# Clustered attention and a routed expert layer on one core: four places in a hand-written order of work are moved

## The chip, the cores and the metric

The kernel runs on one core of one Trainium2 chip. A core has a matrix engine (TensorE, PE in the profile; its weight loads are PEld), VectorE (DVE), ScalarE (ACT), GpSimd (POOL) and SyncE (SP), which here only issues DMA transfers. Each engine works through its own list of instructions in order and waits at an instruction until the semaphores that it needs have come. TensorE writes to PSUM, which VectorE and ScalarE read. Times are device microseconds (us) of one launch, lower is better.

## The reference

The first half is attention over clusters. For each of 4 batches and 8 heads (768 tokens, 64 columns a head), each query and each key is given to the most similar of 16 centroids, and a query may look only at keys of its own cluster:

```python
q_assign = np.argmax(np.einsum('bhsd,hcd->bhsc', q_n, c_n), axis=-1)
k_assign = np.argmax(np.einsum('bhsd,hcd->bhsc', k_n, c_n), axis=-1)
mask = q_assign[:, :, :, None] == k_assign[:, :, None, :]
scores = scale * np.matmul(q, k.transpose(0, 1, 3, 2))
scores = np.where(mask, scores, -1000000000.0)
scores = scores - np.max(scores, axis=-1, keepdims=True)
attn = np.exp(scores)
attn = attn / (np.sum(attn, axis=-1, keepdims=True) + 1e-09)
return np.matmul(attn, v).astype(np.float32)
```

The second half takes the 3072 rows of 512 columns that come out. Rows with a positive `x @ w_skip` go to one of 8 experts (the largest of `x @ w_gate`), a two-layer network with 1024 hidden columns, and `gate * result` is added to the row; the others pass unchanged. All data are float32.

## The kernel before, in words

**Pairs and tiles.** Two heads of one batch make a *pair*, so there are 16 pairs (0 to 15). A pair has 24 *score tiles*: 2 halves of 384 queries, 6 blocks of 128 keys, 2 heads. "Tile 7.16" is tile 16 of pair 7, counted from 0. For a tile, `score` issues two products into a PSUM tile `ps` (lines L553 and L554: the rounded high parts and mask rows, and the low-part corrections), ScalarE takes the exponential into `PT` (L556), and GpSimd adds the `PT` of a half up in `acc` (L561, L567; the last pair of them on VectorE). There are two `ps` buffers, so tile n can only start when the exponential of tile n-2 is done. Twice in a half, six `PT` at a time, `avs` multiplies by V into one PSUM tile `av` (L578, six products that the trace counts as 12, called an av block here). A pair's blocks stand behind its tiles 7 and 13 (first half) and 19 and the next pair's tile 1 (second half). When a half is through, `vm` and `oT` (L591, L592) are the reading of `av` by ScalarE; there is a single `av` buffer, so the next half's first block waits for it.

**What is prepared for later pairs.** Between the tiles stands the work for the next two or three pairs:

- `load` (L346): the `raw` tile, Q and K transposed, 768 KB, two buffers; `load_v` (L354) loads V.
- `sims` (L431): similarities to the centroids, copied to `ss` (L438 on ScalarE, L436 on VectorE for the first pair).
- `assign`: five VectorE steps on `ss` turned round (L462 on TensorE): largest (L444), equal (L447), weight (L450), largest weight (L453), and the one-hot rows `oh` (L455). The generator yields between them, and numbers of the table say how many tiles lie between.
- `masks`: the *mask product*, three small products of `oh` (L474), ScalarE's scaling into `mk` (L478), and eight DMAs of 24 KB (L486) that put 16 rows each into `QM` (queries) and `KB` (keys): four for `QM`, then four for `KB`.
- `split_hi` (L376, L379): rounded high parts `hi`, and DMAs of 192 KB into rows 0 to 63 of `QM` and `KB`; `split_lo` (L386) and `copies` (L395, L396): low parts, and eight DMAs into `qc` and `kc`.
- `smax` (L515, L517): before the scores of a pair, the largest score of every query. 24 products `sm`, one beside nearly every score tile, each reduced by VectorE into `M`; three `sm` buffers. The first of a pair needs the `hi` rows and the mask rows of `QM` and `KB`.
- `mneg` (L528), `mrows` (L536, L541): the *maxima's rows*. VectorE joins the maxima in `MX`, TensorE turns them round, ScalarE writes them into two rows of both `QM` (L541, twice).
- `sums`, `recip`, `xout` (L602 with `sr` L605; L613 with `rs` L618; L639 with `x` L644 and `out` L653): the sums of the previous pair, their reciprocals, and its output turned round, scaled and stored.

The small products (`sims`, `sums`, `mrows`, `recip`, `xout`, `assign`, `masks`, routing) share a PSUM pool `x_ps` of two buffers: such a product waits until the reader of the tile two before it is done. In pairs 5, 9 and 13 (and 4, 8, 12) routing work of the batch before stands in between as well, mostly VectorE's.

**What sets the order.** Nothing is scheduled by the machine. `tasks` gives each function a place in tiles relative to its pair, from the table `PLAN`; `FIRST` replaces some numbers for the first three pairs. `steps` takes the tasks in order of these places and issues their instructions, so a larger number puts an instruction further down the list of its engine. A `yield` inside a function puts the rest of it down later by that many tiles. `zero_rows` sets rows 64 to 95 of four `QM` tiles to zero once, before the first pair.

The expert half follows (L1018 to L1181): gathers of rows by indirect DMA, and three products each for hidden and output layers. The change touches no line of it.

Of the kernel before, what the change touches and what calls it, by code (L numbers as in the profile page):

```python
# [12 lines left out]
F32 = mybir.dt.float32  # L13
# [4 lines left out]
AF = mybir.ActivationFunctionType  # L18
ALU = mybir.AluOpType
# [24 lines left out]


PLAN = {
    "load": -60.0, "load_v": -45.0, "weights": 72.0, "sims": -42.9, "assign": (-34.45, 0.07, 0.04, 0.04, 0.04, 1.6),
    "hi": (-34.3, -28.3), "masks": (-31.1, 0.6), "lo": (-28.35, -16.35), "copies": -16.3, "smax": (-21.1, 1.0, -0.4),
    "mneg": (-9.0, 3.2), "mrows": ((-4.5, 0.2, 0.05), (5.5, 0.8, 0.3)),
    "av": 1.6, "acc": 25.62, "sums": 29.2, "recip": 31.5, "xout": ((31.52, 0.1), (43.55, 0.08)),  # L50
    "tail": ((16.0, 16.6, 19.2), (28.5, 28.6, 29.3)),
    "route": (29.25, 34.9, 58.9), "early": (86.5, 100.9),
    "rtail": ((5.3, 10.9, 16.2, 17.5, 21.5, 18.2, 23.6, 24.2), (5.35, 10.92, 29.1, 29.2, 29.4, 29.5)),
# [6 lines left out]
FIRST = {  # L60
    0: {
        "load_v": -18.9, "sims": -20.0, "hi": (-19.9, -19.8, -19.7, -19.6), "assign": (-19.0, 0.1, 0.01, 0.01, 0.01, 0.01),
        "lo": (-18.7, -18.6, -16.9, -16.8), "masks": -17.0, "smax": (-14.0, 0.1, 13.0, 0.75), "mneg": (-12.85, 8.7),
        "mrows": ((-12.8, 0.1, 0.0), (9.2, 0.0, 0.0)),
    },
    1: {
        "sims": -42.2, "hi": (-42.4, -42.3), "lo": (-40.1, -40.0), "copies": -39.9, "assign": (-36.83, 13.2, 1.3, 1.3, 1.3, 1.3),
        "masks": (-17.6, 0.1), "smax": (-14.5, 1.0, 0.0, 0.92), "mneg": (-2.3, 8.2), "mrows": ((-1.6, 0.1, 0.2), (8.8, 0.3, 0.3)),
    },
    2: {  # L70
        "smax": (-16.0, 0.95, 0.0), "mneg": (-5.2, 6.3), "mrows": ((-4.5, 0.2, 0.05), (7.4, 0.3, 0.3)),
    },
}

# [3 lines left out]
class Kernel:  # L78
# [203 lines left out]
    def tasks(self, i):  # L282

        p, last = {**PLAN, **FIRST.get(i, {})}, i == self.npair - 1
        r = [(s, lambda s=s: self.score(i, s)) for s in range(NS)]
        add = lambda t, f, *a: r.append((t, lambda: f(i, *a)))
        if i:
            add(p["load"], self.load)
        add(p["load_v"], self.load_v)
        if i in (1, 2):  # L290
            add(-20.1 - i * NS, self.zero_rows)
        add(p["sims"], self.sims)
        add(p["assign"][0], self.assign, *p["assign"][1:])
# [12 lines left out]
        for n in range(24):
            add(t0 + dt * n if n < 12 else t0 + 12 * dt + gap + dt2 * (n - 12), self.smax, n)
        for hf in range(2):
            add(p["mneg"][hf], self.mneg, hf)
            add(p["mrows"][hf][0], self.mrows, hf, *p["mrows"][hf][1:])  # L310
            for g in range(0, KT, GROUP):
                add(12 * hf + 2 * (g + GROUP) + p["av"], self.avs, hf, range(g, g + GROUP))
        if not last:
            add(p["sums"], self.sums, (0, 1))
            add(p["recip"], self.recip)
            for hf in range(2):
                add(p["xout"][hf][0], self.xout, hf, p["xout"][hf][1])
        else:
            for hf in range(2):
                t = p["tail"][hf]  # L320
                add(t[0], self.sums_last, hf)
                add(t[1], self.recip_last, hf)
                add(t[2], self.xout_last, hf)
        if i == self.npair - HP - 1:
            for t, f in zip(p["early"], (self.early_lists, self.early_rows)):
                add(t, f)
        if last:
            for hf in range(2):
                ts = p["rtail"][hf]
# [26 lines left out]
    def zero_rows(self, i):  # L356

        for a in range(2):
            self.nc.vector.memset(self.QM[i][a].bitcast(F32)[64:96, :], 0.0)

    def operands(self, i):
        c = self.st[i]
# [206 lines left out]
    def avs(self, i, hf, kts):  # L569
        c, nc = self.st[i], self.nc  # L570
        if kts[0] == 0:
            c["av"] = self.ps_av.tile([P, HALF + 1], F32, name="av")
        av = c["av"]
        first = None
        for kt in kts:
            for a in range(2):

                nc.tensor.matmul(av[a * D:(a + 1) * D, :], lhsT=c["vt"][:, kt, a * D:(a + 1) * D],  # L578
                                 rhs=self.pt(i, hf * 2 * KT + kt * 2 + a), start=(kt == 0), stop=(kt == KT - 1),
                                 skip_group_check=True)  # L580
                if not first:
                    first = self.newest()
                    self.tc.add_manual_dep(first, c[f"exp{hf}{kts[-1]}"].name, mybir.DependencyInfo(
                        mybir.DependencyClass.Sync, mybir.DependencyReason.DATA), reason="group")
        if kts[-1] == KT - 1:
            if hf == 0:
                c["oT"] = self.work.tile([P, S], F32, name="oT", bufs=5)
            if i < self.npair - 1 or hf == 0:
                yield 1.0
            vm = self.small.tile([P, 1], F32, name="vm")  # L590
            nc.scalar.activation(out=vm, in_=av[:, HALF:], func=AF.Copy)  # L591
            nc.scalar.activation(out=c["oT"][:, hf * HALF:(hf + 1) * HALF], in_=av[:, :HALF],  # L592
                                 func=AF.Identity, bias=vm)
            self.out_mark = self.newest()

    def sums(self, i, hfs):

# [719 lines left out]
```

## Time and profile before

| what | value |
|---|---|
| time, three runs | 743.0 us median (742.95 to 744.28) |
| profiled execution, its own time | 743.75 us |
| its span, first to last instruction | 742.0 us |
| mean granted TensorE clock | 0.976 |
| TensorE busy | 679.9 us, 92% of the span |
| VectorE / ScalarE / GpSimd busy | 72% / 53% / 44% |

The span divides into a start of about 25 us without score tiles, some 495 us with them, about 31 us for most pairs, and some 220 us of experts. In a row of the timeline the first number is the start in us, the second the length; brackets hold the idle time before and what ended it. A wait row reads: engine and instruction that waited, what it waited for, us in total, times, longest. "L474" is line 474 of the kernel before; numbers of the changed file run up to 8 higher from line 594 on.

### The profile page before, as it was taken

The page shows a single profiled execution, that of the slowest core. Times are in us where ns is not written, and L with a number is a line of the kernel's source. Part 1 is how long each engine was busy: PE and PEld are TensorE (multiplying, and loading weights), DVE is VectorE, ACT ScalarE, POOL GpSimd, SP SyncE. Part 2 cuts the span into 40 slices and gives each one's busy share as a digit, 9 for nine tenths or more (in the row PEclk, how much of TensorE's full clock was granted, in tenths as well). Part 3 has the DMA queues.
Part 4 walks back from the last instruction along what each step waited for, and adds up shares of the span by engine and source line. Part 5 has one row for each costly group of instructions (what it writes and reads, how often), then busy time and mean ns, then how long its engine had stood idle before and what let it go on. Part 6 is the DMA issues. An engine that isn't in the chain of part 4 may idle for free. (4 is left out here: it accounts for less than half of the span.)

```text
span 742.0 us, 12111 instructions
## 1 busy us (share of the span) xinstructions
PE 679.9 (92%) x3961; PEld 474.1 (64%) x3961; DVE 531.8 (72%) x1072; ACT 390.5 (53%) x793; POOL 329.7 (44%) x355
## 2 busy tenths in 40 slices
PE   4699999999999999989999999899799999999995
PEld 2455665656556565656665655555578988998883
DVE  7565777758889786888885888885667975667711
ACT  6254556656555565655656555573455455455520
POOL 7455545645456454554564544653342222221001
PEclk9889999999999999999999999999899999999998
DMA  8432647557665475563754653331256666667520
GB/s 224 139 76 65 158 115 201 144 140 189 171 200 134 127 181 122 141 153 102 171 133 113 159 130 95 86 130 36 74 195 218 228 215 237 198 217 243 176 71 29
DMA packets 54351, 110.14 MB, mean 148 GB/s; under 512 B 8615, under 2 KB 22823, under 8 KB 54288
## 3 DMA queue, kind: packets, MB, share of 16 engines
q1 hardware_dynamic: 50832, 101.73, 49.0%
q0 software_dynamic: 2656, 7.24, 2.9%
q8 instruction: 32, 0.52, 0.3%
q10 hardware_dynamic: 800, 0.39, 0.2%
q14 instruction: 31, 0.25, 0.1%
HBM read 61.00 MB, written 10.62 MB: 97 GB/s over the span
## 5 line engine op out<-in xcount | busy, mean ns | idle before, releaser
L556 ACT ACTIVATE PT<-ps 128x384 f32<-128x384 f32 x384 | 183.6, 492 | 187.5 <-PE ps L554 167.9
L517 DVE TENSOR_REDUCE M<-sm 128x1 f32<-128x384 f32 x384 | 205.2, 554 | 92.4 <-PE sm L515 88.4
L567 POOL TENSOR_TENSOR acc<-acc,PT 128x384 f32<-128x384 f32 x217 | 202.0, 951 | 121.2 <-ACT PT L556 121.0
L553 PE MATMUL ps<-QM,KB 98*128 98x384 f32 x384 | 149.8, 390 | 5.3 <-ACT PT L556 3.9
L515 PE MATMUL sm<-KB,QM 96*128 96x384 f32 x384 | 139.4, 369 | 4.8 <-DVE M L517 3.1
L578 PE MATMUL av<-PT,vt 128*64 128x385 f32 x768 | 141.5, 504 | 0.0
L554 PE MATMUL ps<-qc,kc 128*128 128x384 f32 x384 | 132.3, 344 | 0.0
L553 PEld LDWEIGHTS ps<-QM,KB 98*128 98x128 f32 x384 | 73.3, 191 | 57.5 <-ACT PT L556 28.5
L561 POOL TENSOR_TENSOR acc<-PT 128x384 f32<-128x384 f32 x64 | 58.4, 913 | 114.0 <-ACT vm L591 104.0
L515 PEld LDWEIGHTS sm<-KB,QM 96*128 96x128 f32 x384 | 75.5, 197 | 29.4 <-issue 10.9
L578 PEld LDWEIGHTS av<-PT,vt 128*64 128x64 f32 x768 | 50.3, 139 | 60.6 <-issue 60.3
L554 PEld LDWEIGHTS ps<-qc,kc 128*128 128x128 f32 x384 | 74.0, 193 | 0.1
L944 POOL DMA_INDIRECT out<-yo,idw x15 | 19.2, 1281 | 112.5 <-DVE yo L1072 101.0
L1048 PE MATMUL ph<-x2l,w1h 128*128 128x256 f32 x224 | 63.6, 284 | 1.6 <-DVE x2l L1060 1.6
L1049 PE MATMUL ph<-x2h,w1h 128*128 128x256 f32 x224 | 63.5, 284 | 0.0
L1050 PE MATMUL ph<-x2h,w1l 128*128 128x256 f32 x224 | 63.4, 283 | 0.0
L1124 DVE SCALAR_TENSOR_TENSOR hl<-ph,hh 128x256 fp32r<-128x256 f32 x56 | 23.7, 423 | 38.5 <-ACT hh L1123 38.4
L1123 ACT ACTIVATE hh<-ph 128x256 fp32r<-128x256 f32 x56 | 21.5, 383 | 47.9 <-PE ph L1050 47.8
L1048 PE MATMUL py<-w2l,hh 128*128 128x512 f32 x112 | 45.1, 403 | 0.0
L1048 PEld LDWEIGHTS ph<-x2l,w1h 128*128 128x128 f32 x224 | 42.9, 192 | 2.1 <-DVE x2l L1060 1.8
L1050 PE MATMUL py<-w2h,hl 128*128 128x512 f32 x112 | 43.7, 390 | 0.0
L1049 PE MATMUL py<-w2h,hh 128*128 128x512 f32 x112 | 43.7, 390 | 0.0
(260 smaller groups left out, 1003.9 us busy)
## 6 DMA issues: line engine op xcount, KB each, us to landing
wraw<-w SPq DMA_DIRECT2D x72, 512.0 KB, 4.6
raw<-qk SPq DMA_DIRECT2D x16, 768.0 KB, 5.5
vt<-v SPq DMA_DIRECT2D x16, 384.0 KB, 4.2
QM<-hi SPq DMA_DIRECT2D x30, 192.0 KB, 6.4
KB<-hi SPq DMA_DIRECT2D x30, 192.0 KB, 3.1
kc<-hi SPq DMA_DIRECT2D x30, 192.0 KB, 3.6
kc<-raw SPq DMA_DIRECT2D x30, 192.0 KB, 3.4
qc<-hi SPq DMA_DIRECT2D x30, 192.0 KB, 3.6
```

The source lines that it names most:

```text
L515: nc.tensor.matmul(sm, lhsT=c["qm"][a][0:96, j * P:(j + 1) * P], rhs=c["kb"][a][0:96, hf * HALF:(hf + 1) * HALF], start=True, stop=True)
L517: nc.vector.tensor_reduce(out=c["m"][:, j, a, hf:hf + 1], in_=sm, axis=AX.X, op=ALU.max)
L553: nc.tensor.matmul(ps, lhsT=c["kb"][a][0:98, ks], rhs=c["qm"][a][0:98, sl], start=True, stop=False)
L554: nc.tensor.matmul(ps, lhsT=c["kc"][a][:, ks], rhs=c["qc"][a][:, sl], start=False, stop=True)
L556: nc.scalar.activation(out=pt, in_=ps, func=AF.Exp, scale=D ** -0.5)
L561: nc.gpsimd.tensor_tensor(out=acc, in0=self.pt(i, s - 2)[:, :HALF], in1=pt, op=ALU.add)
L567: (nc.vector if dve else nc.gpsimd).tensor_tensor(out=acc, in0=acc, in1=pt, op=ALU.add)
L578: nc.tensor.matmul(av[a * D:(a + 1) * D, :], lhsT=c["vt"][:, kt, a * D:(a + 1) * D], rhs=self.pt(i, hf * 2 * KT + kt * 2 + a), start=(kt = ...
L1048: nc.tensor.matmul(ps, lhsT=ah, rhs=bl, start=first, stop=False)
L1049: nc.tensor.matmul(ps, lhsT=ah, rhs=bh, start=False, stop=False)
L1050: nc.tensor.matmul(ps, lhsT=al, rhs=bh, start=False, stop=last)
L1124: nc.vector.scalar_tensor_tensor(out=hl[:, f, :], in0=ph, scalar=0.0, in1=hh.bitcast(F32)[:, f, :], op0=ALU.max, op1=ALU.subtract)
```

## The change

Six edits, in the program's words; nothing is added to or taken from what is computed:

1. `PLAN["assign"]`: the last step (`oh`, L455) is yielded 4.8 tiles instead of 1.6 after the fourth; `PLAN["masks"]`: the mask product goes from place -31.1 to -27.05, and ScalarE's `mk` follows 0.3 instead of 0.6 tiles later. In a pair this is from tile 16 to tile 20.
2. `PLAN["oT"]`: reading `av`. For the first half `vm` and `oT` come 4.5 tiles after the last av block instead of 1.0, still on ScalarE. For the second half `vm` stays on ScalarE, and `oT` becomes a VectorE instruction (add of a scalar per row), 3.55 tiles after the block. The last pair's second half is as before.
3. `PLAN["mrows"]`: the second half's maxima's rows are written 0.1 and 0.05 tiles after their product, not 0.8 and 0.3.
4. `FIRST[2]["load"]`: the third pair's `raw` is requested at place -64.75 instead of -60.
5. `FIRST[0]["smax"]`, `["mneg"]`, `["mrows"]`: pair 0's second twelve maxima come 0.6 instead of 0.75 tiles apart, and what follows them about a tile sooner.
6. `zero_rows` is issued on GpSimd, not on VectorE, and five tiles later.

```diff
-    "load": -60.0, ... "assign": (-34.45, 0.07, 0.04, 0.04, 0.04, 1.6),
-    ... "masks": (-31.1, 0.6), ...
-    "mneg": (-9.0, 3.2), "mrows": ((-4.5, 0.2, 0.05), (5.5, 0.8, 0.3)),
-    "av": 1.6, "acc": 25.62, ...
+    "load": -60.0, ... "assign": (-34.45, 0.07, 0.04, 0.04, 0.04, 4.8),
+    ... "masks": (-27.05, 0.3), ...
+    "mneg": (-9.0, 3.2), "mrows": ((-4.5, 0.2, 0.05), (5.5, 0.1, 0.05)),
+    "av": 1.6, "oT": (4.5, 3.55), "acc": 25.62, ...
@@ FIRST
-    0: ... "smax": (-14.0, 0.1, 13.0, 0.75), "mneg": (-12.85, 8.7), "mrows": ((-12.8, 0.1, 0.0), (9.2, 0.0, 0.0)),
+    0: ... "smax": (-14.0, 0.1, 13.0, 0.6), "mneg": (-12.85, 7.55), "mrows": ((-12.8, 0.1, 0.0), (8.2, 0.1, 0.0)),
-    2: "smax": (-16.0, 0.95, 0.0), ...
+    2: "load": -64.75, "smax": (-16.0, 0.95, 0.0), ...
@@ tasks
-            add(-20.1 - i * NS, self.zero_rows)
+            add(-15.0 - i * NS, self.zero_rows)
@@ zero_rows
-            self.nc.vector.memset(self.QM[i][a].bitcast(F32)[64:96, :], 0.0)
+            self.nc.gpsimd.memset(self.QM[i][a].bitcast(F32)[64:96, :], 0.0)
@@ avs, behind the last block of a half
-            if i < self.npair - 1 or hf == 0:
+            last, oT = i == self.npair - 1, c["oT"][:, hf * HALF:(hf + 1) * HALF]
+            if not last or hf == 0:
                 yield 1.0
             vm = self.small.tile([P, 1], F32, name="vm")
-            nc.scalar.activation(out=vm, in_=av[:, HALF:], func=AF.Copy)
-            nc.scalar.activation(out=c["oT"][...], in_=av[:, :HALF], func=AF.Identity, bias=vm)
+            if not last and hf:
+                nc.scalar.activation(out=vm, in_=av[:, HALF:], func=AF.Copy)
+                yield p[hf] - 1.0
+                nc.vector.tensor_scalar(out=oT, in0=av[:, :HALF], scalar1=vm, scalar2=None, op0=ALU.add)
+            else:
+                if not last:
+                    yield p[hf] - 1.0
+                nc.scalar.activation(out=vm, in_=av[:, HALF:], func=AF.Copy)
+                nc.scalar.activation(out=oT, in_=av[:, :HALF], func=AF.Identity, bias=vm)
```

**Place one: ScalarE, from tile 8.19 to tile 9.6.** `QM_172` and `QM_173` are the two query tiles of the pair that gets its maxima's rows, `PT` the exponentials, `ex` a step of the routing. Before:

```order
L541 ACTIVATE QM_172<-x_ps 2x384
L541 ACTIVATE QM_173<-x_ps 2x384
L556 ACTIVATE PT<-ps 128x384 x7
L591 ACTIVATE vm<-av 128x1
L592 ACTIVATE oT<-av,vm 128x384
L556 ACTIVATE PT<-ps 128x384 x3
L438 ACTIVATE ss<-x_ps 128x384
L605 ACTIVATE sr<-x_ps 128x384
L556 ACTIVATE PT<-ps 128x384
L802 ACTIVATE ex<-ex 128x48
L541 ACTIVATE QM_172<-x_ps 2x384
L541 ACTIVATE QM_173<-x_ps 2x384
```

And with the change:

```order
L541 ACTIVATE QM_172<-x_ps 2x384
L541 ACTIVATE QM_173<-x_ps 2x384
L556 ACTIVATE PT<-ps 128x384 x2
L478 ACTIVATE mk<-x_ps,mbias,mscale 128x384
L556 ACTIVATE PT<-ps 128x384 x5
L594 ACTIVATE vm<-av 128x1
L556 ACTIVATE PT<-ps 128x384 x3
L438 ACTIVATE ss<-x_ps 128x384
L613 ACTIVATE sr<-x_ps 128x384
L541 ACTIVATE QM_172<-x_ps 2x384
L541 ACTIVATE QM_173<-x_ps 2x384
L556 ACTIVATE PT<-ps 128x384
```

`mk` now stands between the exponentials of tiles 21 and 22, `oT` of the second half is gone from ScalarE, and the second pair of `QM` rows stands directly behind `sr`, in front of one exponential and of `ex`.

**Place two: TensorE and SP around the mask product of pair 9, in pair 7.** TensorE before, from tile 7.16 on (`QM_176` and `KB_182` are the operands of pair 8's maxima):

```order
L553 MATMUL ps<-QM_174,KB_180 128x384
L554 MATMUL ps<-qc_2526,kc_2528 128x384
L515 MATMUL sm<-KB_182,QM_176 128x384
L474 LDWEIGHTS oh
L474 MATMUL x_ps<-ident_bf,oh 128x128
L474 LDWEIGHTS oh
L474 MATMUL x_ps<-ident_bf,oh 128x128
L474 LDWEIGHTS oh
L474 MATMUL x_ps<-ident_bf,oh 128x128
L553 MATMUL ps<-QM_175,KB_181 128x384
```

TensorE with the change, from the av block behind tile 7.19 on:

```order
L578 MATMUL av<-PT,vt 64x385 x6
L553 MATMUL ps<-QM_174,KB_180 128x384
L554 MATMUL ps<-qc_2526,kc_2528 128x384
L515 MATMUL sm<-KB_183,QM_177 128x384
L474 LDWEIGHTS oh
L474 MATMUL x_ps<-ident_bf,oh 128x128
L474 LDWEIGHTS oh
L474 MATMUL x_ps<-ident_bf,oh 128x128
L474 LDWEIGHTS oh
L474 MATMUL x_ps<-ident_bf,oh 128x128
L553 MATMUL ps<-QM_175,KB_181 128x384
```

SP's list of transfers in the same stretch of a later pair, before:

```order
L379 DMA QM_176<-hi 64x768
L379 DMA QM_177<-hi 64x768
L486 DMA QM_176<-mk 16x384 x2
L486 DMA QM_177<-mk 16x384 x2
L486 DMA KB_182<-mk 16x384 x2
L486 DMA KB_183<-mk 16x384 x2
L379 DMA KB_182<-hi 64x768
L379 DMA KB_183<-hi 64x768
L653 DMA out<-x 128x3x128
L354 DMA vt<-v 128x768
```

And with the change:

```order
L379 DMA QM_176<-hi 64x768
L379 DMA QM_177<-hi 64x768
L379 DMA KB_182<-hi 64x768
L379 DMA KB_183<-hi 64x768
L661 DMA out<-x 128x3x128
L486 DMA QM_176<-mk 16x384 x2
L486 DMA QM_177<-mk 16x384 x2
L486 DMA KB_182<-mk 16x384 x2
L486 DMA KB_183<-mk 16x384 x2
L354 DMA vt<-v 128x768
```

The product moved past four tiles and an av block, and the eight transfers of mask rows moved behind the two of `KB`'s `hi` rows and one store.

**Place three: SP at the start, the copies of pair 1 and the third `raw`.** `kc_295` and `qc_293` are pair 1's low-part operands for the first head. Before:

```order
L379 DMA KB_180<-hi 64x768
L379 DMA KB_181<-hi 64x768
L395 DMA kc_295<-hi 64x768
L396 DMA kc_295<-raw 64x768
L395 DMA qc_293<-hi 64x768
L396 DMA qc_293<-raw 64x768
L395 DMA kc_296<-hi 64x768
L396 DMA kc_296<-raw 64x768
L395 DMA qc_294<-hi 64x768
L396 DMA qc_294<-raw 64x768
L346 DMA raw<-qk 128x1536
L354 DMA vt<-v 128x768
```

And with the change:

```order
L379 DMA KB_180<-hi 64x768
L379 DMA KB_181<-hi 64x768
L346 DMA raw<-qk 128x1536
L395 DMA kc_293<-hi 64x768
L396 DMA kc_293<-raw 64x768
L395 DMA qc_291<-hi 64x768
L396 DMA qc_291<-raw 64x768
L395 DMA kc_294<-hi 64x768
L396 DMA kc_294<-raw 64x768
L395 DMA qc_292<-hi 64x768
L396 DMA qc_292<-raw 64x768
L354 DMA vt<-v 128x768
```

The load moved in front of eight copies. In the changed program it waits for the readers of the first `raw`, of which GpSimd's subtraction (L414) is the last.

More of the change, by code (lines that the diff above doesn't have):

```diff
@@ L46 @@
 PLAN = {
-    "load": -60.0, "load_v": -45.0, "weights": 72.0, "sims": -42.9, "assign": (-34.45, 0.07, 0.04, 0.04, 0.04, 1.6),
-    "hi": (-34.3, -28.3), "masks": (-31.1, 0.6), "lo": (-28.35, -16.35), "copies": -16.3, "smax": (-21.1, 1.0, -0.4),
-    "mneg": (-9.0, 3.2), "mrows": ((-4.5, 0.2, 0.05), (5.5, 0.8, 0.3)),
-    "av": 1.6, "acc": 25.62, "sums": 29.2, "recip": 31.5, "xout": ((31.52, 0.1), (43.55, 0.08)),
+    "load": -60.0, "load_v": -45.0, "weights": 72.0, "sims": -42.9, "assign": (-34.45, 0.07, 0.04, 0.04, 0.04, 4.8),
+    "hi": (-34.3, -28.3), "masks": (-27.05, 0.3), "lo": (-28.35, -16.35), "copies": -16.3, "smax": (-21.1, 1.0, -0.4),
+    "mneg": (-9.0, 3.2), "mrows": ((-4.5, 0.2, 0.05), (5.5, 0.1, 0.05)),
+    "av": 1.6, "oT": (4.5, 3.55), "acc": 25.62, "sums": 29.2, "recip": 31.5, "xout": ((31.52, 0.1), (43.55, 0.08)),
     "tail": ((16.0, 16.6, 19.2), (28.5, 28.6, 29.3)),
@@ L62 @@
         "load_v": -18.9, "sims": -20.0, "hi": (-19.9, -19.8, -19.7, -19.6), "assign": (-19.0, 0.1, 0.01, 0.01, 0.01, 0.01),
-        "lo": (-18.7, -18.6, -16.9, -16.8), "masks": -17.0, "smax": (-14.0, 0.1, 13.0, 0.75), "mneg": (-12.85, 8.7),
-        "mrows": ((-12.8, 0.1, 0.0), (9.2, 0.0, 0.0)),
+        "lo": (-18.7, -18.6, -16.9, -16.8), "masks": -17.0, "smax": (-14.0, 0.1, 13.0, 0.6), "mneg": (-12.85, 7.55),
+        "mrows": ((-12.8, 0.1, 0.0), (8.2, 0.1, 0.0)),
     },
@@ L70 @@
     2: {
-        "smax": (-16.0, 0.95, 0.0), "mneg": (-5.2, 6.3), "mrows": ((-4.5, 0.2, 0.05), (7.4, 0.3, 0.3)),
+        "load": -64.75, "smax": (-16.0, 0.95, 0.0), "mneg": (-5.2, 6.3), "mrows": ((-4.5, 0.2, 0.05), (7.4, 0.3, 0.3)),
     },
@@ L585, in avs @@
         if kts[-1] == KT - 1:
+            p = PLAN["oT"]
             if hf == 0:
                 c["oT"] = self.work.tile([P, S], F32, name="oT", bufs=5)
-            if i < self.npair - 1 or hf == 0:
+            last, oT = i == self.npair - 1, c["oT"][:, hf * HALF:(hf + 1) * HALF]
+            if not last or hf == 0:
                 yield 1.0
             vm = self.small.tile([P, 1], F32, name="vm")
-            nc.scalar.activation(out=vm, in_=av[:, HALF:], func=AF.Copy)
-            nc.scalar.activation(out=c["oT"][:, hf * HALF:(hf + 1) * HALF], in_=av[:, :HALF],
-                                 func=AF.Identity, bias=vm)
-            self.out_mark = self.newest()
+            if not last and hf:
[7 more added lines that the diff above has]
+                nc.scalar.activation(out=oT, in_=av[:, :HALF], func=AF.Identity, bias=vm)
+                self.out_mark = self.newest()
     def sums(self, i, hfs):
```

## The prediction

> **What bounds the kernel now.** I read the page first, then the list of waits by TensorE, then the timeline at the places that the change touches. A wait row gives the engine and its instruction, what ended the wait, us in total, times, longest.
>
> ```profile
> span 742.0 us, 12111 instructions
> ...
> PE x_ps L474 <- DVE oh L455: 9.1, 15, 0.9
> ...
> PE x_ps L639 <- ACT QM L541: 6.0, 9, 0.7
> ...
> PE x_ps L431 <- DMA raw<-qk: 5.4, 1, 5.4
> ...
> PE x_ps L536 <- DVE MX L528: 3.3, 5, 2.1
> ...
> PE x_ps L639 <- DVE rs L618: 3.0, 5, 0.7
> ...
> PE sm L515 <- DMA KB<-hi: 1.5, 3, 0.7
> ```
>
> TensorE is the busy engine, so in the attention part its own waits are what the end can gain from. The first three rows are 20.5 us, and each stands at an instruction that the change moves or feeds sooner. The other engines' waits are far longer and cost nothing by themselves. What a removed wait is worth depends on what is late next: ScalarE (an exponential for every tile) or VectorE (a reduction for every tile).
>
> **The change, part by part.** All terms are against the profiled execution (743.75 us: the span of 742.0 and 1.75 around it); the median of the runs, 743.0, lies 0.75 below it.
>
> *Start.* The timeline, start and length; in the two rows of windows the fields behind the length are the busy time of PE, PEld, DVE, ACT and POOL with counts, the granted TensorE clock, the DMA share and GB/s.
>
> ```profile
> 6.02 1.93 PE L431 MATMUL x_ps<-raw,cb 128*32 128x384 f32 x8 [0.86 <-DVE cb L227]
> 6.67 3.12 DVE L359 MEMSET QM<- 32x768 f32 x4 [0.20 <-issue]
> 16.75 6.28 DVE L517 TENSOR_REDUCE M<-sm 128x1 f32<-128x384 f32 x12 [0.48 <-PE sm L515]
> 18.24 1.81 POOL L414 TENSOR_TENSOR kc<-raw,kc 64x768 fp32r<-64x768 f32 x1
> 20.13 3.60 POOL L386 TENSOR_TENSOR raw<-raw,hi 128x768 fp32r<-128x768 f32 x2
> 27.20 1.68 POOL L561 TENSOR_TENSOR acc<-PT 128x384 f32<-128x384 f32 x2 [3.47 <-ACT PT L556]
> 28.98 0.55 SPq L346 DMA_DIRECT2D raw<-qk  x1
> 34.78 1.51 PE L431 MATMUL x_ps<-raw,cb 128*32 128x384 f32 x8 [5.39 <-DMA raw<-qk]
> 39.26 2.48 SPq L486 DMA_DIRECT2D QM<-mk  x4
> 44.82 0.34 PE L553 MATMUL ps<-QM,KB 98*128 98x384 f32 x1
> 30.60:34.80 4.20, 0.02 (x3) 0.05 (x4) 0.56 (x2) 0.00 (x0) 0.74 (x1) 0.51 0.83 287
> 34.80:42.50 7.70, 7.54 (x31) 3.59 (x32) 2.08 (x4) 2.15 (x4) 1.85 (x2) 0.60 0.06 16
> ```
>
> The first pair's similarities end at 7.95, but VectorE's copy of them stands behind the four memsets, which end at 9.79. On GpSimd the memsets leave that copy free: **−1.8** (bounds 0, if GpSimd, where no memset of this size is shown, holds up something, and −1.8). Their cover is GpSimd's idle 3.47 us ahead of its first sums at 27.20. It is of much the same length as VectorE's 3.12 us for them; if each took twice as long, the sums would start some 3 us later, and nothing on TensorE waits for those.
>
> The third load is issued at 28.98 behind eight copies that wait for GpSimd's subtraction L386 (to 23.73); TensorE then stands 5.39 us at the similarities that need it. In the new order it needs only L414 (to 20.05, less the 1.8), so with the same 5.8 us from issue to landing (28.98 to 34.78) the data lie there near 24, well before TensorE's turn. SP waits at the load until then, and only the eight copies of pair 1 and a load of V are queued behind it, which waited for GpSimd longer before. The wait goes, and so does the cause of the low clock behind it: 0.60 granted over 7.7 us is about 3.1 us lost. Together that is 8.5 us. VectorE takes part of it back: tile 10 of pair 0 at 44.82 needs the mask rows of pair 1, these VectorE's one-hots, and ahead of those stand nine reductions at 6.28/12 = 0.52 and the five one-hot steps. I put the tile at about 39.8: **−5.0** (−3.5, if VectorE's queue leaves the rows only that much sooner, to −8.5). Pair 0's second maxima, issued a little closer together, are part of this stretch: each is the same product and the same 0.52 of VectorE, so they add no work, and I give them no term of their own.
> [...]
>
> *The mask product, in each pair.* Tiles 16 and 20 of pair 7, whose stretch is an ordinary one:
>
> ```profile
> 265.78 0.44 PE L553 MATMUL ps<-QM,KB 98*128 98x384 f32 x1
> 267.15 0.34 PE L474 MATMUL x_ps<-ident_bf,oh 128*128 128x128 bf16 x3 [0.57 <-DVE oh L455]
> 272.02 0.44 PE L553 MATMUL ps<-QM,KB 98*128 98x384 f32 x1
> 265.82 0.58 ACT L592 ACTIVATE oT<-av,vm 128x384 f32<-128x384 f32 x1
> 268.38 0.67 ACT L478 ACTIVATE mk<-x_ps,mbias,mscale 128x384 fp32r<-128x384 f32 x1
> 274.00 1.02 ACT L556 ACTIVATE PT<-ps 128x384 f32<-128x384 f32 x2 [0.24 <-PE ps L554]
> 265.97 1.12 DVE L455 TENSOR_TENSOR oh<-wts,mwc 128x384 bf16<-128x384 f32 x1
> ```
>
> The one-hots (1.12) are issued after the same reduction as before, so at the product's new place, four tiles and an av block (together 5 us) later, they are long there. The stretch 16 to 20 (6.24 us) loses the 0.57 and the product's own 0.15: −0.7, and a little more since `oT` no longer stands in front of an exponential. The product now falls in tiles 20 to 24, where ScalarE has 1.26 us for two exponentials of 1.02: with `mk`'s 0.67 in that loop about 0.45 comes out again, beside the 0.15. Net −0.1 in each of 11 ordinary pairs: **−1.1** (−9 if ScalarE gives nothing back, +1 if the next exponentials are late too).
>
> *Pairs 5, 9 and 13*, where routing loads VectorE:
>
> ```profile
> 204.36 0.44 PE L553 MATMUL ps<-QM,KB 98*128 98x384 f32 x1
> 206.77 0.34 PE L474 MATMUL x_ps<-ident_bf,oh 128*128 128x128 bf16 x3 [0.94 <-DVE oh L455]
> 213.22 0.44 PE L553 MATMUL ps<-QM,KB 98*128 98x384 f32 x1
> 206.90:209.50 2.60, 2.60 (x13) 2.25 (x12) 2.15 (x5) 1.66 (x4) 1.84 (x3) 0.75 0.87 304
> 209.50:213.20 3.70, 3.70 (x18) 1.82 (x17) 1.98 (x3) 1.86 (x4) 1.53 (x2) 0.72 0.81 222
> ```
>
> Tiles 16 to 20 take 8.86 us here against 6.24. The wait of 0.94 is part of it, the clock behind it the rest: 0.25 × 2.60 + 0.28 × 3.70 = 1.7. If the wait is what lets the clock fall, a pair gains up to 2.6; three of them, pair 9 less: **−5.0** (−1, if another short wait lowers the clock, to −7). [...]
>
> *`oT` of the second half, off ScalarE.*
>
> ```profile
> 280.16 0.44 PE L553 MATMUL ps<-QM,KB 98*128 98x384 f32 x1 [0.26 <-ACT PT L556]
> ...
> 279.15 0.58 ACT L592 ACTIVATE oT<-av,vm 128x384 f32<-128x384 f32 x1
> ```
>
> The score behind it waited 0.26 for the exponential that `oT` held up; with the lost overlap −0.35 a pair. Against it stands a wait that the late mask rows make. `mk` ends some 4.6 us later, about 273.6 in pair 7, and the first maxima product needs the fifth transfer:
>
> ```profile
> QM<-hi SPq DMA_DIRECT2D x30, 192.0 KB, 6.4
> ...
> QM<-mk SPq DMA_DIRECT2D x60, 24.0 KB, 4.3
> KB<-mk SPq DMA_DIRECT2D x60, 24.0 KB, 1.9
> ```
>
> Four issues of 2.48/4 = 0.62 and a landing of 1.9 make 278.0, about when TensorE comes there: I take +0.3 in 13 pairs. If it waits, everything of TensorE is queued behind it, the next score first, and ScalarE waits for that score. On SP the store of the second output half now stands ahead of the mask rows and waits for VectorE's scaling, which in its list stands right behind the one-hots and so is done before `mk`. The 1.5 us of waits for the `hi` rows of `KB` end, since these now go ahead of the mask rows. Net −0.35 × 13 + 0.3 × 13 − 1.5 is about −2; with VectorE's added 0.55 for `oT` I take **−1.4** (−5 to +3). In pair 1 that 0.55 stands ahead of maxima that are late already (the 3.3 us row of waits): **+0.5** (0 to 1).
>
> *The maxima's rows behind the sums*, pair 8:
>
> ```profile
> 254.53 0.49 PE L613 MATMUL x_ps<-ident,sr 128*128 128x128 f32 x3
> 255.70 0.55 PE L639 MATMUL x_ps<-ident,oT 128*128 128x128 f32 x3 [0.68 <-ACT QM L541]
> 254.27 0.49 ACT L556 ACTIVATE PT<-ps 128x384 f32<-128x384 f32 x1 [0.50 <-PE ps L554]
> 254.78 0.86 ACT L541 ACTIVATE QM<-x_ps 2x384 fp32r<-2x384 f32 x2
> ```
>
> The output product waits for a buffer of `x_ps` until the second `QM` write ends (255.64). These two writes now stand ahead of the exponential, 0.49 sooner, and ScalarE had 0.50 idle there. 0.68 in nine pairs, and three of the waits for `rs` (5, 9, 13): 6.0 + 2.1 is 8.1, less 0.6 for the exponentials behind them: **−7.5** (−8.1 to −3, if the exponential, 0.86 later, makes a score wait instead).
>
> The sum: −1.8 − 5.0 − 1.1 − 5.0 − 1.4 + 0.5 − 7.5 = **−21.3**, so 722.4 as a profiled execution and **721.7** as a median.
>
> **The rivals.**
>
> *ScalarE gives it back.* Only the start gains, and what TensorE no longer waits for at L474 and L639 it waits for at exponentials. For it: a loop of 1.26 us holds 1.02 of exponentials, and `mk` or the `QM` writes don't fit into the rest. Against it: those waits were only 0.26 at 280.16, and ScalarE is idle 0.50 just before the writes. −6.8 from the start and −1 for the rest give about 735.
>
> *Everything without a price.* −8.5 at the start, −9 and −7 at the mask product, −8.1 at the rows: with −1.8 some −34, so about 709. For it speaks that the covers are long; against it the loops of ScalarE and VectorE that take up slack within a tile.
>
> *Slower: the mask rows come too late.* The first maxima product of a pair waits for the rows of `KB`, and TensorE with it. When the small transfers stand behind large ones they land 4.3 us after issue (the `QM` rows, behind `hi` rows of 192 KB that take 6.4), not 1.9. In the new order `hi` rows of `KB` and a store go right ahead. Then +2.4 × 13 = +31 on my sum, about 753. It decides from a wait of about 0.3 + 21/13 = 1.9 us in each pair on. Against it: the `KB` rows behind the same queue landed in 1.9, and the large ones are issued some 3 us earlier than the small.
> [...]
>
> *No change to speak of*: the gains are covered by waits for late reductions of VectorE, which gets `oT` (0.55 a pair); about 743.
>
> **How the numbers follow.** Chances: the forecast 0.62, ScalarE's rival 0.19, no price 0.05, slower 0.10, no change 0.04. A measurement of this kernel can tell about 0.2%, 1.5 us, from no change. The forecast, ScalarE's and the no-price case are all faster: 0.86; within 0.2% 0.04; slower 0.10. The range is 711 to 738: at its lower end half of the open bounds come in, at its upper end ScalarE's case with a few us more.
>
> **What would show it.** Right: the similarities at L431 without a wait and a granted clock near 1.00 between 30 and 42 us; the waits of L474 for `oh` and of L639 for `QM` gone; tiles 16 to 20 near 5.5 us in ordinary pairs and near 6.5 in pairs 5, 9 and 13; tiles 20 to 24 near 3.1 instead of 2.5. Wrong: maxima products that wait over 1.9 us for `KB` rows, many new waits of scores for exponentials around tiles 8 and 22, or low clock in the same three pairs though the wait is gone.

## The result, and the profile after

The changed kernel took 720.1 us (median of four runs, 718.8 to 724.2) against 743.3 us before (four runs; the table ahead of the prediction has three): a ratio of 0.970, with an interval of 0.966 to 0.974. The prediction was 721.7 us, with a range of 711 to 738. Its profiled execution has a span of 718.5 us.

The page and TensorE's waits of the changed kernel:

```profile
span 718.5 us, 12168 instructions
...
PE 671.8 (94%) x3961; PEld 470.0 (65%) x3961; DVE 525.4 (73%) x1083; ACT 384.3 (53%) x778; POOL 344.9 (48%) x359
```

```profile
PE x_ps L875 <- DVE rhs L870: 5.1, 5, 1.9
...
PE sm L515 <- DMA KB<-mk: 4.3, 4, 1.6
PE x_ps L536 <- DVE MX L528: 4.2, 5, 2.1
...
PE ps L553 <- ACT PT L556: 2.0, 11, 0.3
...
PE x_ps L647 <- DVE rs L626: 0.5, 1, 0.5
...
PE x_ps L474 <- DVE oh L455: 0.3, 1, 0.3
```

The three rows of 20.5 us are gone: the mask product's wait for `oh` is 0.3 instead of 9.1, and the output product (now L647) no longer waits for the second `QM` write, nor the similarities for `raw`. Two rows are longer or new: the first maxima products wait for the mask rows of `KB`, and a routing product (L875) for VectorE's `rhs`, for which this row stood before:

```profile
PE x_ps L867 <- DVE rhs L862: 3.7, 2, 1.9
```

Tiles 16 and 20 of pair 7 again, and the start (timeline; the window rows have the columns named in the prediction, and are of the start, of tiles 16 to 20 of pair 5, and of pair 14):

```profile
250.79 0.45 PE L553 MATMUL ps<-QM,KB 98*128 98x384 f32 x1
...
256.08 0.44 PE L553 MATMUL ps<-QM,KB 98*128 98x384 f32 x1
```

```profile
22.55 0.44 PE L553 MATMUL ps<-QM,KB 98*128 98x384 f32 x1 [0.57 <-ACT QM L541]
...
28.86 0.85 PE L431 MATMUL x_ps<-raw,cb 128*32 128x384 f32 x8
...
36.81 0.42 PE L515 MATMUL sm<-KB,QM 96*128 96x384 f32 x1 [1.63 <-DMA KB<-mk]
37.07 0.34 PE L553 MATMUL ps<-QM,KB 98*128 98x384 f32 x1
```

```profile
30.60:34.80 4.20, 3.87 (x25) 2.26 (x25) 1.85 (x5) 1.70 (x4) 1.87 (x2) 1.00 0.11 31
192.33:198.16 5.83, 5.54 (x31) 3.44 (x31) 5.83 (x12) 4.58 (x10) 5.81 (x6) 1.00 0.74 201
456.60:460.00 3.40, 3.40 (x15) 1.80 (x15) 1.47 (x3) 0.86 (x2) 2.25 (x3) 0.50 0.48 132
```

The stretch 16 to 20 takes 5.29 us (6.24 before). In pair 5 it takes 5.83 at full clock (second window row; 8.86 before). The third window row, in pair 14, is at half clock, where the kernel before was not. Over the whole span half clocks cover 23 us, 36 before. The first tile starts at 22.55, the similarities at 28.86 without a wait, and the clock there is full (first window row). Tile 10 of pair 0 stands at 37.07 instead of 44.82, and what ends last there is now pair 1's mask rows.

The starts of the score tiles of both traces, subtracted stretch by stretch, give where the 23.5 us of the two spans went:

| stretch | forecast, us | measured, us |
|---|---|---|
| up to the first tile | −1.8 | −2.2 |
| pair 0 | −5.0 | −5.9 |
| tiles 16 to 24, nine ordinary pairs | −0.1 each | −0.49 each, −4.4 |
| tiles 16 to 24, pairs 5, 9 and 13 | −5.0 | −6.1 |
| tiles 0 to 5, pairs 3 to 14 | −1.4 | +0.8 |
| tiles 5 to 8, pairs 3 to 14 | −7.5 | −10.7 |
| tiles 8 to 16, pairs 3 to 14 | none | +3.2 |
| tiles 16 to 24 of pair 14 | with the ordinary pairs | +1.6 |
| pair 1 | +0.5 | −0.5 |
| rest of pairs 2 and 15 | none | −0.6 |
| from the last tile on (experts) | none | +1.2 |

The 1.6 us of pair 14 are the half clock shown above. Six other profiles, of kernels with and without the new order, have one or two such windows at the same place, so it belongs to no one edit.

The last row has two parts. From the last tile to the first expert product it took 34.2 to 39.0 us in 14 profiles of these kernels, in no order that follows the edits. From there to the end it took 186.4 to 186.5 us in the eight that lack an edit, and 187.5 to 190.2 in the six that have all of them. The change touches no line there, yet in each of the six one step of the experts is later (`w2l`, `x2l` and `w1l` are low parts of weights and rows), first before, then after:

```profile
556.11 3.07 DVE L1043 TENSOR_TENSOR w2l<-wraw,w2h 128x1024 fp32r<-128x1024 f32 x1 [0.41 <-ACT w2h L1042]
559.57 0.39 PE L1048 MATMUL ph<-x2l,w1h 128*128 128x256 f32 x1 [1.58 <-DVE x2l L1060]
```

```profile
529.88 4.11 DVE L1051 TENSOR_TENSOR w2l<-wraw,w2h 128x1024 fp32r<-128x1024 f32 x1 [0.41 <-ACT w2h L1050]
534.38 0.39 PE L1056 MATMUL ph<-x2l,w1h 128*128 128x256 f32 x1 [2.62 <-DVE x2l L1068]
```

GpSimd's `w1l`, 2.4 us long, began 0.4 us ahead of VectorE's `w2l` before and 1.7 ahead of it now, so that a second one falls into it. `x2l` stands behind `w2l`, TensorE waits 1.0 us more, and in five of the six a half clock begins within a microsecond of that wait's end.

So a single span tells differences of a few us badly. The experiments are therefore read by medians of runs, and by stretches of tiles, which mostly repeat to a few hundredths where no half clock falls in.

### The profile page after: what moved, and what is told of

Read it like the earlier page. It is cut to its first block, busy times and chain, and to the rows that moved or that the text cites. A ratio compares the mean times of both kernels' runs of the same rounds, so it can differ in the third digit from the quotient of the medians.

```text
span 718.5 us, 12168 instructions
## 1 busy us (share of the span) xinstructions
PE 671.8 (94%) x3961; PEld 470.0 (65%) x3961; DVE 525.4 (73%) x1083; ACT 384.3 (53%) x778; POOL 344.9 (48%) x359
## 5 line engine op out<-in xcount | busy, mean ns | idle before, releaser
L567 POOL TENSOR_TENSOR acc<-acc,PT 128x384 f32<-128x384 f32 x217 | 216.8, 1022 | 77.7 <-ACT PT L556 73.0
L553 PE MATMUL ps<-QM,KB 98*128 98x384 f32 x384 | 148.3, 386 | 4.2 <-ACT PT L556 2.0
L561 POOL TENSOR_TENSOR acc<-PT 128x384 f32<-128x384 f32 x64 | 56.2, 889 | 119.2 <-ACT vm L594 66.5
L1051 DVE TENSOR_TENSOR w2l<-wraw,w2h 128x1024 fp32r<-128x1024 f32 x30 | 39.5, 1318 | 8.2 <-ACT w2h L1050 7.5
```

Source lines behind the costliest of these rows:

```text
L553: nc.tensor.matmul(ps, lhsT=c["kb"][a][0:98, ks], rhs=c["qm"][a][0:98, sl], start=True, stop=False)
L561: nc.gpsimd.tensor_tensor(out=acc, in0=self.pt(i, s - 2)[:, :HALF], in1=pt, op=ALU.add)
L567: (nc.vector if dve else nc.gpsimd).tensor_tensor(out=acc, in0=acc, in1=pt, op=ALU.add)
L1051: lo_engines[k].tensor_tensor(out=l[:, cs], in0=w[k][:, cs], in1=h.bitcast(F32)[:, cs], op=ALU.subtract)
```

## The experiments

### Each part alone

**The rows behind the sums.**

```diff
-    "mrows": (..., (5.5, 0.8, 0.3)),
+    "mrows": (..., (5.5, 0.1, 0.05)),
```

> Only the maxima's rows right behind the sums (0.1 and 0.05 instead of 0.8 and 0.3), all else as before. The trace of the changed kernel is 0.88 us shorter between tiles 5 and 8 in each of pairs 3 to 14. If all of that belongs to this edit: 12 x 0.88 = -10.6, about 732.7. By the step of the prediction (the waits of the output product alone): -7.5, about 735.8. By the rival that ScalarE gives it back at the exponentials behind: -3 at most, 740 or more.

736.2 us, a ratio of 0.987 (0.981 to 0.992). Tiles 5 to 8 are 0.86 to 0.89 us shorter in every one of pairs 3 to 14, −10.6 in all, and no exponential behind makes a score late. Tile 7 of pair 8 in this kernel (TensorE, ScalarE; the prediction's rows are from tile 7 of pair 7):

```profile
283.20 0.49 PE L613 MATMUL x_ps<-ident,sr 128*128 128x128 f32 x3
283.53 0.49 PE L639 MATMUL x_ps<-ident,oT 128*128 128x128 f32 x3
...
282.40 0.86 ACT L541 ACTIVATE QM<-x_ps 2x384 fp32r<-2x384 f32 x2
283.29 0.87 ACT L556 ACTIVATE PT<-ps 128x384 f32<-128x384 f32 x2
```

From one product to the next it is now 0.33 us; before it was 1.17 (254.53 to 255.70) in pair 7 and 1.15 in pair 8. That is 0.84 for a wait whose row says 0.68: without the wait the second product starts 0.16 us before the record of the first one ends. The `QM` writes go where ScalarE was idle (0.50 in the row at 254.27 before).

**The mask product four tiles later.**

```diff
-    "assign": (..., 1.6),  "masks": (-31.1, 0.6),
+    "assign": (..., 4.8),  "masks": (-27.05, 0.3),
```

> Only the one-hots' last step and the mask product four tiles later, all else as before. By the prediction's steps: -1.1 in the ordinary pairs and -5.0 in pairs 5, 9 and 13, about 737.2. From the two traces: tiles 16 to 20 lose 0.72 (wait and product) and tiles 20 to 24 gain 0.45 in an ordinary pair, -3.0 in eleven; -6.1 in pairs 5, 9, 13; +3 for first maxima products that wait for the mask rows of the keys: -6, about 737. If the full 0.94 by which tiles 16 to 20 are shorter comes from this edit alone, -8.5, about 734.8. If the low clock in pairs 5 and 13 has another cause than the wait for the one-hots, it is still there (0.50 for 3.4 us behind tile 16) and the time is near 741.

742.9 us, 0.997 (0.994 to 0.999): next to nothing. The 9.1 us of waits for `oh` are gone here too, and tiles 16 to 24 of pairs 5, 9 and 13 are 2.4, 0.9 and 2.4 us shorter. But an ordinary stretch 16 to 20 is only 0.44 shorter, which tiles 20 to 24 give back (+0.45). Pair 7, TensorE and ScalarE:

```profile
267.92 0.44 PE L553 MATMUL ps<-QM,KB 98*128 98x384 f32 x1 [0.26 <-ACT PT L556]
...
266.91 0.58 ACT L592 ACTIVATE oT<-av,vm 128x384 f32<-128x384 f32 x1
267.39 0.86 ACT L556 ACTIVATE PT<-ps 128x384 f32<-128x384 f32 x2
```

With TensorE 0.7 us sooner, `oT` stands in the way of the exponential that the second score behind needs: a wait that was hidden behind the old one. The 5.7 us of pairs 5, 9 and 13 hardly show in the time either. In this profile pair 14 is 3.0 longer with two windows of half clock, which the kernel with the start alone has there too, and pairs 0 and 1 are 3.9 longer. How much of the 5.7 an average run keeps stays open; the medians show 1.9.

**The reading of `av`.**

```diff
-            if i < self.npair - 1 or hf == 0:
-                yield 1.0
 ...
+                yield p[hf] - 1.0
+                nc.vector.tensor_scalar(out=oT, in0=av[:, :HALF], scalar1=vm, ...)
```

> Only the reading of av: first half later on ScalarE, second half's last step on VectorE. By the prediction's step without the mask rows' wait: -0.35 in 13 pairs and +0.5 in pair 1, -4.0, about 739.3. From the traces: tiles 16 to 20 lose 0.22 (0.94 less wait and product), tiles 2 to 5 up to 0.3, twelve pairs: -6, about 737. Rival: the 0.55 us that VectorE gets in each pair makes reductions late by as much: no change, 743.

750.5 us, 1.009 (1.006 to 1.012): slower. Tiles 2 to 5 lose the 0.4 us, as the traces said. But tiles 5 to 8 of pairs 5, 9 and 13 take 0.6, 1.3 and 3.0 us more. Pair 9 (`ex` has a VectorE step, L808, and a ScalarE step, L810), TensorE, ScalarE and VectorE:

```profile
317.05 0.55 PE L647 MATMUL x_ps<-ident,oT 128*128 128x128 f32 x3 [2.08 <-ACT QM L541]
...
315.89 0.24 ACT L810 ACTIVATE ex<-ex 128x48 f32<-128x48 f32 x1 [1.19 <-DVE ex L808]
316.14 0.86 ACT L541 ACTIVATE QM<-x_ps 2x384 fp32r<-2x384 f32 x2
...
311.80 0.61 DVE L596 TENSOR_SCALAR oT<-av,vm 128x384 f32<-128x384 f32 x1
...
314.98 0.87 DVE L808 TENSOR_TENSOR ex<-L,mxe 128x48 f32<-128x48 f32 x1
```

`oT` on VectorE stands ahead of the routing's chain, `ex` of the routing on ScalarE waits for that chain, the `QM` writes stand behind `ex`, and the output product waits 2.08 us for them. The 0.6 in pair 5 is as long as `oT` (0.61). In pairs 9 and 13 VectorE's `ex` also takes 0.87 instead of 0.20, behind an addition on GpSimd that began 0.12 to 0.14 us ahead of it, and in pair 13 a half clock follows. In ordinary pairs tiles 16 to 20 are 0.22 longer: `mk`, still there, puts the first half's later `oT` off until the av block waits for it:

```profile
270.28 2.16 PE L578 MATMUL av<-PT,vt 128*64 128x385 f32 x12 [0.16 <-ACT oT L601]
```

This profile is of the fastest of the six runs (746.4), so its rows show where time is lost, and not all of the 5.7 us that the medians give.

**The start**, all three edits, and the load alone:

```diff
     2: {
-        "smax": (-16.0, ...
+        "load": -64.75, "smax": (-16.0, ...
```

> Only the start: third load ahead of pair 1's copies, zeroing on GpSimd, pair 0's second maxima closer together. From the traces: first tile 2.2 us sooner, pair 0 5.9 us shorter, -8.1, about 735.2. By the prediction's steps -6.8, about 736.5. If the later pairs take it back through VectorE or the loads: 740 or more.

> Only the third load ahead of pair 1's copies; zeroing stays on VectorE, pair 0's maxima as before. If the load alone is behind the gain in pair 0 (5.39 us of wait and the half clock behind it, less what VectorE takes back): -5.9, about 737.4, with a granted clock of 1.00 from 25 to 42 us. If the mask rows of pair 1 also need pair 0's maxima closer together or VectorE free of the zeroing, tile 10 of pair 0 is only some 3.5 us sooner: about 739.8.

All three: 737.3 us, 0.989 (0.985 to 0.993). The load alone: 734.9 us, 0.990 (0.987 to 0.993). The zeroing on GpSimd and pair 0's closer maxima add nothing that these runs can tell. The first tile starts 2.0 us sooner with them, yet in these two profiles pair 1 does not. Its first tile with all three, and with the load alone:

```profile
36.97 0.42 PE L515 MATMUL sm<-KB,QM 96*128 96x384 f32 x1 [1.61 <-DMA KB<-mk]
...
53.42 0.45 PE L553 MATMUL ps<-QM,KB 98*128 98x384 f32 x1
```

```profile
52.95 0.45 PE L553 MATMUL ps<-QM,KB 98*128 98x384 f32 x1
```

TensorE comes sooner to a maxima product that waits for pair 1's mask rows, and behind that wait the clock was at half for 3.4 us in this profile. With the load alone the clock is full from the first tile up to 68 us. Two profiles with all the start's edits and no half clock in pair 0, those of the changed kernel and of the last kernel below, do start pair 1 sooner, at 51.9 and 51.1. In a second profile of the changed kernel, with two half clocks in pair 0, it starts at 54.5. So the 2 us of the first tile can reach pair 1; where a half clock fell in pair 0 they did not (53.42 and 54.5).

### Two parts together, and all but one

The first and the third edit together:

> The reading of av (which alone made the kernel slower) together with the maxima's rows right behind the sums. Theory: alone, the moved reading held VectorE's chain of the routing in pairs 5, 9 and 13, ScalarE's exponential of the routing waited for it, and the second maxima rows stood behind that on ScalarE; with the rows ahead of it this is gone. Then tiles 5 to 8 lose 0.88 in all of pairs 3 to 14 (-10.6), tiles 2 to 5 lose 0.4 (-4.6), and tiles 16 to 20 still gain 0.22 (+2.7): -12.5, about 731. Rival: the two are independent, the sum of the two alone: -8.6 + 5.8 = -2.8, about 741.

734.6 us, 0.988 (0.984 to 0.991): 9.7 us less than before on the same chip, nearer to the theory's 12.5 than to the 2.8 of the two alone. The 0.6 to 3.0 us of pairs 5, 9 and 13 are gone (tiles 5 to 8 are 0.97 to 0.98 shorter in these), tiles 2 to 5 of pairs 3 to 14 lose 5.5 and tiles 16 to 20 still gain 0.22 each. In this profile half clocks cover 44 us, 36 before, which took some of it back: tiles 8 to 16 are 5.5 us longer, 3.1 of it in pair 14 with a half clock, and 0.8 in each of pairs 6 and 10.

Every edit but the third:

> The changed kernel with the reading of av as before. Theory: the exponential of tile 17 again stands behind that reading, so tiles 16 to 20 lose 0.44 instead of 0.94 and tiles 2 to 5 lose nothing: some +6 in tiles 16 to 20 and up to +4 in tiles 2 to 5, less what of the wait for the keys' mask rows that slack covers (3 us): +5 to +8 against the changed kernel, 725 to 728. Rival: the reading of av is worth what it is alone, slower by 5.8, and the kernel without it is faster: about 714.

725.4 us, 0.973 (0.970 to 0.977), beside 722.9 us and 0.972 (0.969 to 0.975) of the whole change on the same chip. The rival (714) falls. The reading of `av` doesn't cost with the others there. By the medians it brings 2.5 us, half of the least that the theory gave (+5 to +8), and the intervals leave open whether it brings anything. By stretch, tiles 16 to 20 are 0.50 longer without it in each of eight ordinary pairs, as the theory has it. The up to 4 us in tiles 2 to 5 did not come (they stay within 0.1 us in sum), part is returned in tiles 8 to 13 (−0.8 in pairs 6 and 10), and the later step in the experts is absent.

### The mask rows: later, and sooner

In the changed kernel the first maxima product of pairs 1 and 4 to 15 waits 6.8 us in all. For 5.4 of this the profile names the mask rows; the rest are seven waits of about 0.2, for whose end it names something else or nothing. The eight transfers are issued 0.63 us apart, and the product needs the fifth. From issue to landing, in the changed kernel:

```profile
KB<-hi SPq DMA_DIRECT2D x30, 192.0 KB, 5.1
...
QM<-mk SPq DMA_DIRECT2D x60, 24.0 KB, 1.9
KB<-mk SPq DMA_DIRECT2D x60, 24.0 KB, 1.9
```

Two kernels change only the order of the eight (the remarks behind `#` tell them apart):

```diff
-        for t in range(2):
-            for a in range(2):
 ...
-                for hf in range(2):
+        for t, a, hf in ((0,0,0), (0,0,1), (0,1,0), (0,1,1), (1,1,0), (1,1,1), (1,0,1), (1,0,0)):    # later
+        for t, a, hf in ((1,0,0), (0,0,0), (1,0,1), (1,1,0), (0,1,0), (1,1,1), (0,0,1), (0,1,1)):    # as needed
```

> The changed kernel with the four transfers of the keys' mask rows in the opposite order, so that the first maxima product needs the eighth instead of the fifth, 3 x 0.63 = 1.9 us later. This measures the price of the slower rival. If each such us is lost on TensorE: 1.9 x 13 = +24.5, about 744.6, which would be the whole gain. If the score tiles around it hide half: +12, about 732. If the wait is hidden: 720.

764.8 us, 1.031 (1.025 to 1.037): slower than before, and 44 us above a kernel that is the changed one but for a single product (721.0, below), on the same chip. That is nearly twice what was expected. Its waits, one such place, and the two windows behind it (L512 is the maxima product here):

```profile
PE sm L512 <- DMA KB<-mk: 29.7, 13, 4.1
```

```profile
126.85 0.41 PE L512 MATMUL sm<-KB,QM 96*128 96x384 f32 x1 [2.11 <-DMA KB<-mk]
...
128.74 1.51 PE L431 MATMUL x_ps<-raw,cb 128*32 128x384 f32 x8
```

```profile
126.80:128.70 1.90, 1.85 (x9) 1.48 (x9) 1.40 (x4) 0.95 (x2) 0.48 (x1) 1.00 0.92 311
128.80:132.10 3.30, 3.30 (x21) 1.18 (x20) 0.64 (x2) 1.41 (x3) 2.06 (x3) 0.50 0.45 140
```

29.7 − 6.8 = 23 us are waits, as computed. The other part is the clock: behind 10 of these 13 waits it is at half for one or two windows of 3.41 us, up to 1.7 us each. This profile is of the fastest of five runs (757.8); the others have a lower granted clock, 0.945 to 0.950 against 0.960.

> The changed kernel with the eight transfers of mask rows in the order in which the maxima products need them (first head's first half of keys and queries, its second half of keys, then the second head). The first maxima product needs the second transfer instead of the fifth, 3 x 0.63 = 1.9 us sooner. In the changed kernel the first maxima product of pairs 1 and 4 to 15 waits 6.8 us in all, 0.16 to 1.63 a pair. If TensorE loses all of it: -6 to -7, about 714. If late reductions or exponentials behind it cover the wait: 719 to 720.

717.9 us, 0.966 (0.960 to 0.973); the kernel of the next paragraph, on the same chip and but for one place the changed kernel, took 721.0. By stretch the theory holds: tiles 2 to 8 of pairs 3 to 14 are 6.0 us shorter in all than in the changed kernel, and the product waits in pairs 5 and 7 alone:

```profile
PE sm L512 <- DMA KB<-mk: 1.4, 2, 0.8
```

So the short waits with other names were for mask rows too. The medians give 3.1, half of the 6, and their intervals leave open how much of it a run keeps.

```diff
-SLOTS = (..., 80.9, 82.9, 83.1,
+SLOTS = (..., 80.9, 83.55, 83.75,
```

> The changed kernel with the slot product of the routing (its second line of six small products) one tile later. In the changed kernel it waits 0.63 us for VectorE's rhs in pairs 6, 10 and 14, where tiles 8 to 13 are 0.78 us longer than before. If that wait is all: -0.78 x 3 = -2.3, about 717.8. If it comes back at the next user of the small products' two buffers: no change, 720.

721.0 us, 0.969 (0.963 to 0.975): no change that can be told. Tiles 8 to 16 are 0.48 shorter in the three pairs, 1.4 us, too little for these intervals.

The transfers as needed and the later product together, and the changed kernel itself beside it:

> The changed kernel with the mask rows' transfers in the order of need and the slot product one tile later. In the profiles the first took 5.2 + 0.9 us from tiles 2 to 8 of pairs 3 to 14, the second 0.48 a pair from tiles 8 to 16 in three pairs: -6 - 1.4, about -7 against the changed kernel on the same chip. If short waits that appear elsewhere let the clock fall as often as before: -3.

> The changed kernel itself once more, for comparison with the others on the same chip: 720 us, a ratio of 0.97 to the kernel before.

With both: **715.4 us**, 0.962 (0.959 to 0.965), beside 722.9 us and 0.972 (0.969 to 0.975) of the changed kernel on the same chip. That is −7.5 us, as expected, and faster than both kernels.

## Why the prediction was right, and where its steps were not

The direction, the mechanism and the size came out: the three waits of 20.5 us went, and what came back in other places was made up by overlap and by fewer half clocks. The sum was −21.3, the spans differ by 23.5, the medians by 23.1 (21.4 in the second measurement). Single terms were off by several us and made up for each other, which is luck in the total.

- **The start**: −6.8 forecast, −8.1 in the trace, −7.5 alone by the medians. By the medians the load alone gives as much as the three edits. The step that these runs don't bear out is "the memsets leave that copy free: −1.8". The first tile did come 2 us sooner, but TensorE then waits 1.6 us for pair 1's mask rows, and whether the rest reaches pair 1 differs with where a half clock fell (it starts at 51.1 to 54.5 in the profiles with all three edits and the mask rows not made later, at 52.95 with the load alone).
- **The mask product in ordinary pairs**: the step "Net −0.1 in each of 11 ordinary pairs" was too small, −0.49. "About 0.45 comes out again, beside the 0.15" was 0.45 in all, and the stretch 16 to 20 lost 0.94, not "−0.7, and a little more". The mask product alone gives 0.44 of the 0.94, and the other 0.50 comes only with the reading of `av` moved as well, which the step put down as the "little more". So the runs add what the step did not say: without the reading of `av` moved, this edit is worth nothing there.
- **Pairs 5, 9 and 13**: −5.0 forecast, −6.1 measured, by the mechanism named. Tiles 16 to 20 took 7.3 us without and 8.4 to 8.9 us with a half clock in the kernels that keep the wait, and 5.6 to 6.0 in those that do not. A half clock fell there in 10 of 18 cases with the wait (six profiles, three pairs) and in none of 24 without it. That two of the three pairs were hit in the profile before is chance: with 10 of 18 the term is about −5.6, an estimate from these rows.
- **`oT` and the mask rows**: −1.4 forecast, +0.8 measured. The waits for mask rows were up to 6.8 us, not 0.3 × 13 = 3.9. The rival's premise fell, though: the rows did not stand behind large transfers; those of `QM` now land 1.9 us after issue too, where 4.3 stood before. What is late is `mk` and the issuing of five transfers one by one, 0.63 us apart.
- **The rows behind the sums**: −7.5 forecast, −10.7 measured, and −10.6 alone by the trace. The mechanism was right; the term was mis-sized by the same overlap (0.84 from start to start for a wait of 0.68), and the 0.6 put down for the exponentials behind was not lost.
- **Pair 1**: the +0.5 did not come.
- **Not forecast**: tiles 8 to 16, +3.2. In pairs 6, 10 and 14 the routing's `rhs` on VectorE became longer, and its product waits for it (last section); the later product alone got back 1.4 of it. Nor did the sum have a term for the experts, where the time from the first product to the end grew by 2.7 us in these two profiles.
- **ScalarE's rival** held for the mask product alone in ordinary pairs, where tiles 20 to 24 took back what tiles 16 to 20 gained, and fell for the whole.
- **The slower rival** had its mechanism right and its price too low: mostly 2.1 us of waiting in each of 13 pairs cost more than the whole gain, and behind 10 of these waits the clock was at half. The changed kernel waits 0.5 us a pair there. On a straight line between the two kernels the point from which it decides is about 1.4 us, an estimate; the prediction gave 1.9.
- **Independent terms** were assumed throughout. The medians of the parts alone are −8.6 (rows), −1.9 (masks), +5.7 (`oT`) and −7.5 (start), a sum of −12, and together they gave −23 (−21 in the second measurement). The kernel with two parts and the one without the reading show two links: the reading of `av` needs the rows ahead of `ex`, and the mask product needs the reading out of the exponential's way. The prediction was right partly because it was made for the whole change.

## What to carry to other kernels

A wait's row can understate what its removal is worth where instructions overlap (0.68 for 0.84 here): measure from start to start. Where several waits on one engine sit within a tile of each other, moving one shows the next, so edits of an order have to be priced together, and a part that is slower alone may be needed by the whole. When transfers are issued one after the other by one queue (0.63 us apart here), put first those that the next product needs; here that took 6 us from the stretches of tiles, a quarter of what the whole change did. Half clocks fell in other places from profile to profile (pairs 5 and 13 in one, 5 and 9 in another), so a term that is read from one pair of profiles can be off by a few us.

## What the runs showed of the hardware

**Half clocks behind short waits.** In the attention part half clocks come in windows of 3.41 us or whole multiples of it: in the profile before one of 10.24 us from 30.69 on, in and behind the wait of 5.39, and single ones at 75.07 and 208.19, whose starts are 39 × 3.41 us apart. They followed behind waits of 0.3 to 0.5 and 0.8 to 0.9 us close together in 10 of 18 cases, and behind the 13 waits of mostly 2.1 us of the kernel with late rows in 10, so that a wait of 2 us with one window behind it cost up to 3.7, an estimate (the wait and half of 3.41). Which pair is hit changes from profile to profile: 5 and 13 before, 5 and 9 with the rows alone, 9 with the load alone. No run shows why the clock was at half behind some of these waits and full behind others of the same length.

**VectorE took longer behind the start of a GpSimd instruction.** The one-hots `oh` in an ordinary pair, and GpSimd's additions at the same time, first in the kernel before, then in the changed one:

```profile
265.97 1.12 DVE L455 TENSOR_TENSOR oh<-wts,mwc 128x384 bf16<-128x384 f32 x1
...
265.81 0.87 POOL L561 TENSOR_TENSOR acc<-PT 128x384 f32<-128x384 f32 x1 [2.40 <-ACT vm L591]
```

```profile
225.34 0.55 DVE L455 TENSOR_TENSOR oh<-wts,mwc 128x384 bf16<-128x384 f32 x1
...
224.43 1.00 POOL L567 TENSOR_TENSOR acc<-acc,PT 128x384 f32<-128x384 f32 x1
225.40 1.21 POOL L567 TENSOR_TENSOR acc<-acc,PT 128x384 f32<-128x384 f32 x1
```

The same instruction takes 1.12 us when an addition began 0.16 ahead of it, and 0.55 when it begins as an addition is ending; both times it ends 0.4 to 0.5 after that addition. In the second case the next addition, which begins 0.06 behind `oh`, takes 1.21, where 180 of GpSimd's 217 additions at L567 take 0.85 to 1.04. Before, `oh` took 1.11 or 1.12 in nine ordinary pairs, each time 0.16 behind such a start, and the 0.57 more is as long as the mask product's wait there. Where the mask product is moved without the reading of `av`, `oh` still takes 1.24 to 1.26 in ordinary pairs and the product doesn't wait: it is far enough behind.

The same shows in `rhs` of the routing, a mean of 556 ns before and 1015 now. In tile 10 of pair 6 it took 0.40 us before, where it began 0.05 ahead of an addition, and 1.21 now, where it begins 0.06 behind one:

```profile
L862 DVE TENSOR_TENSOR rhs<-rv,hs 128x240 bf16<-128x240 bf16 x6 | 3.3, 556 | 0.0
```

```profile
L870 DVE TENSOR_TENSOR rhs<-rv,hs 128x240 bf16<-128x240 bf16 x6 | 6.1, 1015 | 0.0
```

The `ex` and `w2l` above go the same way. `ex` took 0.87 us where an addition had begun 0.12 to 0.14 ahead of it, and 0.20 in the kernel before. `w2l` took 3.07 and 4.11 where GpSimd's `w1l` had begun 0.4 and 1.7 ahead, each time ending 1.1 us after the last `w1l`, and 1.21 with no GpSimd instruction beside it (at 560.10 before, at 534.91 now). No run changed the overlap alone: the durations are read from the records, and that the overlap makes them longer is not shown by an experiment.
